# One of three readings of a bit-trick exponential moves from VectorE to GpSimd, with new orders for chunk start, tail and prologue

## The chip, the cores and the metric

The kernel runs on one NeuronCore of a Trainium2 chip. The metric is the device time of one execution in microseconds (us). Engines are named as in the profile: PE (TensorE), DVE (VectorE), ACT (ScalarE), POOL (GpSimd), SP (the engine that issues most DMAs).

## The reference, cut to what matters

```python
xn = layernorm(x)                      # x: 1 x 2048 x 640, no gain, no bias
q = xn @ wq                            # 32 heads of width 20
k, v = xn @ wk, xn @ wv                # one shared key and value head of width 20
p = softmax(q k^T / sqrt(20))          # per head 2048 x 2048, no mask
A = concat_heads(p @ v) @ wo
B = silu(xn @ w1) @ w2                 # hidden width 1728
out = x + A + B                        # bfloat16
```

The 32 x 2048 x 2048 exponentials, 134 million, are the bulk of the elementwise work.

## The kernel before, in words

**Tiling.** The 2048 queries are four chunks (`QC`) of 512 (`QW`). A unit is one head of one chunk; there are 128 units, in 43 groups of three (the last has two). A step is one group against one block of 128 keys, so a group has 16 steps and the kernel 688 (`T`). In a step PE computes the transposed scores (L749): one matmul of 128 keys x 512 queries for each unit, in different row tiles of the array, into three PSUM banks. Two sets of three banks alternate with the step's parity, so step t cannot start before the exponentials of step t-2 have read their banks.

**Two kinds of exponential.** ACT takes exp of the first two units of a step in one instruction (L767, 128x1024, PSUM to a ring of 31 blocks in SBUF). The third unit is either done by ACT too (then the instruction is 128x1536) or, in what is called a DVE step here, by a bit trick on DVE. The scores arrive scaled and offset such that, rounded to int16, they are the bits of a bfloat16 near the exponential. L781, named `p1`, clamps them to 0..32512 and stores int16 in Z. This piecewise linear exponential is read three times at shifted phases and the readings are averaged: Z itself, Z + 43 and Z + 86 (`PH`), all three reinterpreted as bfloat16. The two sums are written to Y by L842, one instruction for each sum over up to three blocks of Z (`ZB`), issued by `flush_z`; the weights of the three readings are folded into copies of V. `want_dve` (from step 8 on) chooses the kind: a step is a DVE step if the backlog of DVE, as the planner has it, is below `DVE_TH`.

**P times V.** L830 multiplies V with the exponentials into one PSUM bank (bank 6), 32 rows for each unit, four column tiles side by side: units 0 and 1, the first reading of unit 2, and its second reading. A step that is all ACT leaves the fourth place free, and `host` gives it to one waiting third reading. Other third readings are collected by threes into extra instruction blocks (`PT`) of four matmuls. At the end of a group DVE copies the bank to SBUF (L945), a DMA transposes it, four small POOL operations add its parts (L912, L915, L917 twice), DVE takes the reciprocal (L922), and POOL multiplies (L931).

**The other work** runs as jobs in bank 7 between the steps: `h_job` (L1057; one hidden block of the FFN, then tanh on ACT L1065 and a multiply on DVE L1070), `out_job` (L1119 is x W2 of the FFN, L1124 is the product with wo, whose results DVE adds in L1136, L1142 or L1148), and `qd_job` (L1023; queries for the next chunk, spread to their places by DMAs). `fill_chunk` lists the jobs of a chunk: the output products of the chunk before it (`fs`), the hidden blocks (`hs`), the FFN output blocks (`ys`), with a query job after every second one, and gives each a first step, spread evenly. Jobs are taken in this order, the head of the list alone. The `fs` read the transposed attention output of the chunk before, which `try_oT` requests by DMA when its last head is done.

**Who sets the order.** `Sched` is a planner that runs while the kernel is built: it simulates the five engines with a time for every operation, commits the order of each engine, and emits semaphore waits. On the chip each engine runs its list strictly in order. `lock` makes the planner keep POOL's group operations and L842 apart in its own time; no semaphore enforces it. `step` chooses PE's next work: scores when ready, else P times V or a job. `fill` inserts matmuls on zeros (L673, L686) when PE has room and its recent busy share is below `FILL_BELOW`.

**Prologue.** x arrives in 16 tiles, mean and variance come from DVE (L1352) or, for tiles in `ACT_STATS`, from ACT; a Newton iteration gives 1/sigma; `norm` normalizes (L1377 on DVE or POOL, L1372 on ACT, by `NORM_ENG`); tiles in `DT` are transposed by DMA on SP's queue (L1430), the others by PE (`tr_job`, L1450) with an evacuation by DVE (L1461). `PRO` lists the order of transposes (t), keys (k), values (v) and queries (q, d). Fourteen DVE operations of 128x512 (L1441) fill the query tiles with their offset.

**Tail.** After the last step come the remaining P times V blocks, a small transpose on PE (L957), the last products with wo for four row tiles in halves (L1124), PE's transposes of the last 128 attention columns (L1097) with an evacuation (L1102), eight matmuls (L1124) and eight additions on DVE (L1148), each pair followed by an output DMA (L1152). The output buffer `ost` has three slots; the last row tile takes the slot of the third before it.

Of the kernel before, what the change touches and what calls it, by code (L numbers as in the profile page):

```python
# [47 lines left out]
ZB = 3  # L48
ZWAIT = 6
SWITCH = 0.105  # L50
S_LEAD = 0.56
PV_PRESS = 8
DVE_TH = 3.2
# [4 lines left out]
FILL_BELOW = 0.78  # L58
OVER = 0.1
FLUSH_G = 0  # L60
NOD = 0
PV_HOLD = 11
# [267 lines left out]
class Job:  # L330
    def __init__(self, name, mms, reads, consume, gate=None, min_step=-1, banks=None, on_start=None, width=0):
# [8 lines left out]
        self.width = width  # L340


class Builder:
# [17 lines left out]
    def alloc(self):  # L361
# [41 lines left out]
        self.eps = sb([P, 1], F32)  # L403
        self.zero = sb([P, 512], BF16)
# [27 lines left out]
    def steps_init(self):  # L432
# [26 lines left out]
        self.nqd = 0  # L459
        self.thirds = []  # L460
# [17 lines left out]
    def bank_for_job(self, job=None):  # L478
        if not self.started and (job is None or job.name[0] != "v"):
# [5 lines left out]
        if self.s_next >= self.T and not self.pv_q:  # L485
            banks = [7, 0, 1, 2, 3, 4, 5]
# [62 lines left out]
    def step(self, now):  # L549
# [54 lines left out]
        nxt = min(sr, pv_r, job_r)  # L604
        if choice is None:
# [26 lines left out]
        else:  # L632
            if job is None:
                job = cand.popleft()
                job.bank = self.bank_for_job(job)[1]
                self.cur_job = job
            self.do_mm(job, now, d)
# [11 lines left out]
    def fill(self, now, until):  # L649
# [7 lines left out]
        if room < 0.08 or self.busy_share(now) > FILL_BELOW:  # L657
# [49 lines left out]
    def do_mm(self, job, now, d):  # L707
# [4 lines left out]
        op.work = work  # L712
# [7 lines left out]
    def want_dve(self, t):  # L720
        if t < DVE_FROM or t % KT >= KT - NOD:
# [8 lines left out]
    def do_S(self, t, now):  # L730
# [42 lines left out]
        if dv:  # L773
# [9 lines left out]
            sc.new("dve", t_dve_ps(QW), p1, [("B", bb)], [("Z", zs, zp)], prio=1.0, name=f"p1_{t}")  # L783
        first = kt == 0
# [48 lines left out]
    def flush_z(self):  # L833
# [7 lines left out]
        for k in range(2):  # L841
            sc.new("dve", t_dve_4x(w), lambda v, k=k: v.tensor_scalar(  # L842
# [264 lines left out]
    def out_job(self, c, i, e, step=-1, ffn=True, ks=range(DC), src="xres", dst="ost", hmax=H):  # L1107
# [14 lines left out]
        for k in ks:  # L1122
            def f(pe, b, k=k, m=len(mms)):
                return pe.matmul(self.bk(b, 0, 320), self.oT[:, k, i * P:(i + 1) * P],  # L1124
                                 self.wo[:, k, e0:e0 + 320], start=(m == 0), stop=(m == tot - 1))
            mms.append((t_mm(320), f))

        def consume(b):
            ps = self.bk(b, 0, 320)
            rk = ("xres", i, e) if src == "xres" else ("yx", i, e)  # L1130
            in1 = (self.xres if src == "xres" else self.yx)[:, i, e0:e0 + 320]
# [15 lines left out]
            sl = n % 3  # L1147
# [440 lines left out]
```

The softmax here doesn't subtract the row's maximum and nothing guards it: scores larger than these inputs give would overflow.

## Time and profile before

| what | us |
|---|---|
| median of 3 runs (743.72 to 744.91) | 744.6 |
| the profiled execution, its own time | 747.35 |
| its span from first to last instruction | 745.6 |
| PE, DVE, ACT, POOL busy | 721.1, 713.9, 707.9, 111.7 |
| first exponential starts | 15.7 |
| last exponential ends | 733.3 |

Busy times are those of the records. Records of one engine overlap: a 128x1024 exponential has a record of 1.08 us, and the next instruction starts 0.905 us after it. So three engines that are all busy 95% of the time may still have room, and where this matters the spacing from start to start is used, read from the trace's start times.

### The profile page before, as it was taken

To read this page: it belongs to the slowest core of one execution; us is meant where nothing else is said; L and a number is where in the kernel's file an instruction comes from. 1 tells how busy PE (TensorE), PEld (TensorE's weight loads), DVE (VectorE), ACT (ScalarE), POOL (GpSimd) and SP (SyncE) were. 2 spreads that over 40 slices of the span, in tenths; PEclk is the share of its full clock that TensorE was granted. 3 is DMA by queue.
4 is the path that set the end of the run, shared out by engine and by line. 5 is a ranking of instruction groups with operands and counts; after the bars stand their busy time and mean duration, and the time that the engine had idled before them with its cause. 6 is when DMAs were issued, how large, how long until landed. Compare 5 with 4: busy or idle time off the path is not lost.

```text
span 745.6 us, 17784 instructions
## 1 busy us (share of the span) xinstructions
PE 721.1 (97%) x6781; PEld 230.5 (31%) x6781; DVE 713.9 (96%) x1397; ACT 707.9 (95%) x780; POOL 111.7 (15%) x280
## 2 busy tenths in 40 slices
PE   8889999999999999999999999999999999999996
PEld 4332222233332222223333232222333322233332
DVE  7978999999999999999999999999999999999997
ACT  8968999999999999999999999999999999999962
POOL 5421112011112111110120111111111121111100
PEclk9979999999999999999999999999999999999999
DMA  6660000101003110000011211000002110000021
GB/s 188 158 248 15 17 20 16 22 16 15 9 15 62 52 46 16 9 16 1 8 16 25 70 44 37 16 8 8 10 8 43 51 45 8 8 9 8 9 43 36
DMA packets 55961, 27.05 MB, mean 36 GB/s; under 512 B 43686, under 2 KB 55238, under 8 KB 55878
## 3 DMA queue, kind: packets, MB, share of 16 engines
q1 hardware_dynamic: 54566, 25.87, 13.7%
q8 instruction: 55, 0.90, 0.5%
q10 hardware_dynamic: 1312, 0.05, 0.1%
q14 instruction: 28, 0.23, 0.1%
HBM read 11.36 MB, written 2.62 MB: 19 GB/s over the span
## 4 chain that ended last, share of the span: by engine, by line
PE 51%; DVE 20%; ACT 19%; issue 5%; POOL 2%; DMA 2%; DVEq 0%; ACTq 0%; POOLq 0%; SPq 0%
ACT sbt L767 18%; PE psall L830 17%; PE psall L749 17%; DVE sbt L781 9%; PE psall L1057 6%; PE psall L1119 5%; DVE sbt L842 5%; PE psall L1023 2%; PE psall L1124 2%; PE psall L673 2%; DVE sbt L1070 1%; DMA sbt<-sbt 1%; ACT sbt L1065 1%; DVE sbt L945 1%; DVE sbt L1352 1%
## 5 line engine op out<-in xcount | busy, mean ns | idle before, releaser
L767 ACT ACTIVATE sbt<-psall 128x1024 bf16<-128x1024 f32 (+2 forms) x688 | 674.4, 1117 | 21.7 <-PE psall L749 18.1
L781 DVE TENSOR_SCALAR sbt<-psall 128x512 int16<-128x512 f32 x608 | 406.4, 684 | 16.5 <-PE psall L749 10.2
L749 PE MATMUL psall<-sbt 32*128 32x512 bf16 x2048 | 269.5, 385 | 12.0 <-ACT sbt L767 6.0
L830 PE MATMUL psall<-sbt 128*32 128x512 bf16 x3434 | 264.7, 387 | 0.0
L842 DVE TENSOR_SCALAR sbt<-sbt 128x1536 int16<-128x1536 int16 (+2 forms) x436 | 223.9, 533 | 1.5
L749 PEld LDWEIGHTS psall<-sbt 32*128 32x128 bf16 x2048 | 69.7, 91 | 252.8 <-issue 86.8
L830 PEld LDWEIGHTS psall<-sbt 128*32 128x32 bf16 x3434 | 67.2, 95 | 112.4 <-issue 75.1
L915 POOL CAST sbt<-sbt 128x168 f32<-128x168 bf16 x42 | 17.3, 411 | 522.0 <-DMA sbt<-sbt 522.0
L1119 PE MATMUL psall<-sbt 128*128 128x320 bf16 x448 | 86.8, 303 | 0.0
L1057 PE MATMUL psall<-sbt 128*128 128x512 bf16 (+1 forms) x280 | 83.6, 384 | 1.6 <-DVE sbt L1070 1.0
L1119 PEld LDWEIGHTS psall<-sbt 128*128 128x128 bf16 x448 | 34.0, 97 | 43.4 <-issue 34.8
L1070 DVE SCALAR_TENSOR_TENSOR sbt<-sbt,psall 128x512 bf16<-128x512 bf16 (+1 forms) x56 | 38.2, 682 | 1.6 <-ACT sbt L1065 0.8
L931 POOL TENSOR_TENSOR sbt<-sbt 128x240 bf16<-128x240 f32 (+2 forms) x44 | 27.9, 635 | 65.7 <-DVE sbt L922 51.1
L1065 ACT ACTIVATE sbt<-psall 128x512 bf16<-128x512 f32 (+1 forms) x56 | 37.6, 671 | 0.0
L1124 PE MATMUL psall<-sbt 128*128 128x320 bf16 x160 | 31.6, 303 | 1.0 <-DVE sbt L1102 0.7
L1057 PEld LDWEIGHTS psall<-sbt 128*128 128x128 bf16 (+1 forms) x280 | 19.6, 98 | 41.3 <-issue 23.3
L945 DVE CAST sbt<-psall 128x512 bf16<-128x512 f32 x43 | 29.4, 684 | 0.9 <-PE psall L830 0.9
L1023 PE MATMUL psall<-sbt 128*128 128x512 bf16 (+1 forms) x95 | 28.4, 385 | 0.0
L917 POOL TENSOR_TENSOR sbt<-sbt 128x44 f32<-128x44 f32 x84 | 26.9, 320 | 6.6
L673 PE MATMUL psall<-sbt 128*32 128x512 bf16 (+9 forms) x86 | 26.6, 389 | 0.0
L912 POOL TENSOR_TENSOR sbt<-sbt 128x84 f32<-128x84 bf16 x42 | 18.0, 429 | 0.0
L1124 PEld LDWEIGHTS psall<-sbt 128*128 128x128 bf16 x160 | 12.0, 97 | 16.6 <-issue 11.7
(85 smaller groups left out, 198.4 us busy)
## 6 DMA issues: line engine op xcount, KB each, us to landing
sbt<-in_A_x_dram SPq DMA_DIRECT2D x32, 160.0 KB, 3.5
out_dram<-sbt SPq DMA_DIRECT2D x16, 160.0 KB, 1.8
sbt<-in_B_w_dram SPq DMA_DIRECT2D x5, 432.0 KB, 5.3
sbt<-sbt SPq DMA_DIRECT2D x105, 20.0 KB
sbt<-in_B_w_dram SPq DMA_DIRECT2D x13, 160.0 KB, 3.7
sbt<-sbt SPq DMA_TRANSPOSE x67, 2.5
sbt<-in_A_wo_dram SPq DMA_DIRECT2D x5, 160.0 KB, 6.1
sbt<-in_A_wq_dram SPq DMA_DIRECT2D x5, 140.0 KB, 3.6
```

Of the source, the lines that this page charges most:

```text
L673: return pe.matmul(self.bk(UBANK, 0, n, 0, 32), self.zero[:, 0:32], self.zero[:, 0:n], start=False, stop=False, tile_position=(0, 0), skip ...
L749: ins = pe.matmul(self.bk(par3 + j), self.kT[r:r + SLOT, kk, kt * P:(kt + 1) * P], self.qT[r:r + SLOT, h // 4, (x // H) % 2, :], start=Tru ...
L767: return a.activation(self.E[:, b0 * QW:(b0 + na) * QW], self.ps[:, par3 * BANK:(par3 + na) * BANK], AF.Exp, scale=ACT_SCALE)
L781: return v.tensor_scalar(self.Z[:, zs, zp * QW:(zp + 1) * QW], self.bk(bb), 0.0, ZMAX, ALU.max, ALU.min)
L830: return pe.matmul(self.bk(UBANK, 0, QW, q * SLOT, (q + 1) * SLOT), self.v[:, w, kt, :], x, start=start, stop=stop, tile_position=(0, q * ...
L842: sc.new("dve", t_dve_4x(w), lambda v, k=k: v.tensor_scalar(self.Y[:, zs, k, 0:n * QW], Z, float(PH[k + 1][0]), None, ALU.add), zk, [("Y", ...
L1023: return pe.matmul(self.bk(b, 0, QW, 0, rows), self.wq[:, k, lo:hi], self.xnT[:, k, c * QW:(c + 1) * QW], start=(k == 0), stop=(k == DC - 1))
L1057: return pe.matmul(self.bk(b, 0, QW, 0, rows), self.w1[:, k, fk * P:fk * P + rows], self.xnT[:, k, c * QW:(c + 1) * QW], start=(k == 0), s ...
L1065: sc.new("act", t_act(QW), lambda a: a.activation(t, src, AF.Tanh, scale=0.5), [("B", b)], [("tb", tp)], prio=X_PRIO, name=f"th{c}_{fk}")
L1070: sc.new("dve", t_dve_ps(QW), lambda v: v.scalar_tensor_tensor(out=self.hT[0:rows, fk, :], in0=t, scalar=1.0, in1=src, op0=ALU.add, op1=AL ...
L1119: return pe.matmul(self.bk(b, 0, 320), self.hT[0:rows, fk, i * P:(i + 1) * P], self.w2[0:rows, fk, e0:e0 + 320], start=(m == 0), stop=(m = ...
L1124: return pe.matmul(self.bk(b, 0, 320), self.oT[:, k, i * P:(i + 1) * P], self.wo[:, k, e0:e0 + 320], start=(m == 0), stop=(m == tot - 1))
```

## The change

1. **Third reading.** The sum Z + 86 is no longer the second instruction of `flush_z`. For each DVE step POOL adds the int32 constant 86 x 65537 to Z read as 256 int32 words a partition (two packed int16 values each; the clamp leaves no carry), as soon as `p1` is done. The planner counts 0.72 us for it, without `lock`, and 0.1 us more for each L842 that remains.
2. **Chunk start.** `fill_chunk` puts four hidden blocks ahead of the output products of the chunk before (`H_FIRST`).
3. **Tail.** P times V goes first in the last 16 steps (`LASTPV`), the last step is no DVE step. For row tiles 2 and 3 a new `hold_job` collects x + FFN by two matmuls with the identity and four of the five products with wo in PSUM banks of their own; the last product goes to the same bank, and ACT evacuates it with a factor of 0.5. Row tiles 0 and 1 go as before; the two kinds alternate. The transposes of the last 128 columns are urgent. The last row tile has an output slot of its own and its DMA goes out on ACT's queue.
4. **Prologue.** New lists `PRO`, `DT`, `ACT_STATS`, `NW_ENG`, `NORM_ENG`. The fourteen L1441 become one POOL operation and two SP DMAs that copy its row 6 and 8 times, ahead of the loads of w1 and wo. The planner counts less PE activity for transposes and value products, and fills below a busy share of 0.95 in the first 64 steps.
5. **Constants**: `DVE_TH`, `PV_PRESS`, `PV_HOLD`.

```diff
+Y_POOL = True
+Y_TIME = 0.72
+Y_LOCK = False
+Y_SLOW = 0.1
+H_FIRST = 4
+NEARLY = 2
+LASTPV = 16
+DVE_LAST = 1
 ZWAIT = 6
 SWITCH = 0.105
 S_LEAD = 0.56
-PV_PRESS = 8
-DVE_TH = 3.2
+PV_PRESS = 12
+DVE_TH = 2.8
 U_PRIO = 1.1
 X_PRIO = 0.8
 PACE = (0.9, 0.9, 0.9, 0.9)
 WIN = 3.4
 FILL_BELOW = 0.78
+FILL_EARLY = 0.95
+FILL_STEPS = 64
 OVER = 0.1
 FLUSH_G = 0
 NOD = 0
-PV_HOLD = 11
+PV_HOLD = 9
 Q_EVERY = 2
 DT_ISSUE = 1.28
 UT_ISSUE = 1.05
-DT = (4, 5, 6, 7, 11, 12, 13, 14, 15)
-NORM_P = 0.05
+DT = (4, 5, 8, 9, 10, 11, 12, 13, 14, 15)
+NORM_P = 0.5
 DVE_FROM = 8
-PRO = "v0 t8 t9 k2 t10 k3 k4 k5 q1 v1 k6 k7 d0 v2 v3"
-ACT_STATS = (2, 4, 6, 8, 9, 12)
-NW_ENG = ("dve", "pool", "pool", "dve")
-NORM_ENG = ("dve", "act", "dve", "dve", "pool", "pool", "dve", "act", "dve", "pool", "act", "act")
+PRO = "t6 v0 k2 t7 k3 k4 q1 v1 v2 k5 k6 k7 v3 d0"
+ACT_STATS = (4, 6, 9, 12, 14)
+NW_ENG = ("dve", "pool", "dve", "pool")
+NORM_ENG = ("pool", "pool", "pool", "pool", "dve", "act", "act", "dve", "act", "dve", "dve", "act")
...
+        if job is not None and job.use is not None:
+            return 0.0, self.heldb[job.use]
         if not self.started and (job is None or job.name[0] != "v"):
             banks = [7, 6, 5, 4, 3]
         elif not self.pv_started:
             banks = [7, 6]
         else:
             banks = [7]
-        if self.s_next >= self.T and not self.pv_q:
-            banks = [7, 0, 1, 2, 3, 4, 5]
+        if self.s_next >= self.T:
+            banks = [b for b in (7, 0, 1, 2, 3, 4, 5) if b not in self.heldb.values()]
...
+        if self.s_next >= self.T - LASTPV and pv_n:
+            choice = "PV"
...
-        if room < 0.08 or self.busy_share(now) > FILL_BELOW:
+        if room < 0.08 or self.busy_share(now) > (FILL_BELOW if self.s_next > FILL_STEPS else FILL_EARLY):
...
-        op.work = work
+        op.work = min(work, 0.009) if job.name[0] == "v" else min(work, 0.053) if job.name[0] == "t" else work
...
-        if t < DVE_FROM or t % KT >= KT - NOD:
+        if t < DVE_FROM or t % KT >= KT - NOD or t >= self.T - DVE_LAST:
...
+            self.y_on_pool = Y_POOL
+            if self.y_on_pool:
+                c86 = bass.AP(self.c86, self.c86[:, :].offset, [list(self.c86[:, :].ap[0]), [0, QW // 2]])
+                sc.new("pool", Y_TIME, lambda v: v.tensor_tensor(
+                    self.Y[:, zs, 1, zp * QW:(zp + 1) * QW].bitcast(I32),
+                    self.Z[:, zs, zp * QW:(zp + 1) * QW].bitcast(I32), c86, ALU.add),
+                    [("Z", zs, zp), ("c86",)], [("Y", zs, 1, zp)], prio=4.0, name="yp").lock = Y_LOCK
...
-        for k in range(2):
-            sc.new("dve", t_dve_4x(w), lambda v, k=k: v.tensor_scalar(
+        for k in range(1 if self.y_on_pool else 2):
+            sc.new("dve", Y_SLOW + t_dve_4x(w), lambda v, k=k: v.tensor_scalar(
                 self.Y[:, zs, k, 0:n * QW], Z, float(PH[k + 1][0]), None, ALU.add), zk,
...
-            sl = n % 3
-            sc.new("dve", t_dve_ps(320), lambda v: v.scalar_tensor_tensor(
-                out=self.ost[:, sl, e0:e0 + 320], in0=ps, scalar=0.5, in1=in1, op0=ALU.mult, op1=ALU.add),
-                [("B", b), rk], [("ost", sl, e)], prio=X_PRIO, name=f"out{n}_{e}")
+            sl = n % 3 if n < NT - 1 else 3
+            ost = self.ost[:, sl, :] if sl < 3 else self.hT[:, :, :].rearrange("p a b -> p (a b)")[:, 0:D]
+            wk = [("ost", sl, e)] + ([("hT", 0), ("hT", 1)] if sl == 3 else [])
+            if src == "ps":
+                sc.new("act", t_act(320), lambda a: a.activation(ost[:, e0:e0 + 320], ps, AF.Copy, scale=0.5),
+                       [("B", b)], wk, prio=X_PRIO, name=f"out{n}_{e}")
+            else:
+                sc.new("dve", t_dve_ps(320), lambda v: v.scalar_tensor_tensor(
+                    out=ost[:, e0:e0 + 320], in0=ps, scalar=0.5, in1=in1, op0=ALU.mult, op1=ALU.add),
+                    [("B", b), rk], wk, prio=X_PRIO, name=f"out{n}_{e}")
             if e == 1:
-                op = sc.dma("sp", lambda q: q.dma_start(self.outv[:, n, :], self.ost[:, sl, :]),
+                op = sc.dma("act" if sl == 3 else "sp", lambda q: q.dma_start(self.outv[:, n, :], ost),
                             [("ost", sl, 0), ("ost", sl, 1)], [("outd", sl)], P * D * 2, sem=self.s_out[sl])
                 self.out_cnt[sl] += 1
                 op.inc_no = self.out_cnt[sl]
...
+    def hold_job(self, c, i, e):
+        e0 = 320 * e
+        mms = []
+        for m in range(2):
+            def f(pe, b, m=m):
+                return pe.matmul(self.bk(b, 0, 320), self.idb[:, :], self.xres[:, i, e0:e0 + 320], start=(m == 0),
+                                 stop=False)
+            mms.append((t_mm(320), f))
+        for k in range(DC - 1):
+            def f(pe, b, k=k):
+                return pe.matmul(self.bk(b, 0, 320), self.oT[:, k, i * P:(i + 1) * P], self.wo[:, k, e0:e0 + 320],
+                                 start=False, stop=False)
+            mms.append((t_mm(320), f))
+        return Job(f"G{i}_{e}", mms, [("xres", i, e), ("idb",), ("oT", i), ("oTv", c, i), ("wo",)], lambda b: None,
+                   gate=lambda: self.s_next >= self.T and (c, i, e) in self.y_done, hold=(i, e))
...
-        for n, x in enumerate(fs + hs + ys):
+        for n, x in enumerate(hs[:H_FIRST] + fs + hs[H_FIRST:] + ys):
...
-            for i in range(4):
+            for i in range(NEARLY):
                 for e in range(2):
                     self.misc.append(self.out_job(c, i, e, ffn=False, ks=range(DC - 1), src="yx", dst="yx"))
-            self.misc.append(self.oT_last_job(c))
-            for i in range(4):
+            for i in range(NEARLY, 4):
                 for e in range(2):
-                    self.misc.append(self.out_job(c, i, e, ffn=False, ks=range(DC - 1, DC), src="yx"))
+                    self.misc.append(self.hold_job(c, i, e))
+            self.urgent.append(self.oT_last_job(c))
+            fin = [(i, e) for i in range(4) for e in range(2)]
+            lo = [x for x in fin if x[0] < NEARLY]
+            hi = [x for x in fin if x[0] >= NEARLY]
+            while lo or hi:
+                for x, src in ((hi, "ps"), (lo, "yx")):
+                    if x:
+                        i, e = x.pop(0)
+                        self.misc.append(self.out_job(c, i, e, ffn=False, ks=range(DC - 1, DC), src=src))
 
 
     def prologue(self):
@@ -1228,8 +1286,8 @@
         sem = sc.sem
...
+        pool(0.1, lambda g: g.memset(self.c86[:, :], PH[2][0] * 65537), [], [("c86",)])
...
+        pool(0.95, lambda g: g.tensor_scalar(self.tb[:, 0, :], self.zero[:, 0:QW], self.offq[:, :], 1.0, ALU.add, ALU.mult),
+             [("zero",), ("offq",)], [("tb", 0)])
+        tb = self.tb[:, 0, :]
+        for par in range(2):
+            h0 = 2 if par == 0 else 0
+            rep = bass.AP(self.tb, tb.offset, [list(tb.ap[0]), [0, HT - h0], list(tb.ap[1])])
+            op = sc.dma("sp", lambda q, par=par, h0=h0, rep=rep: q.dma_start(self.qT[:, h0:HT, par, :], rep), [("tb", 0)],
+                        [("qb", par, h) for h in range(4 * h0, H)], P * (HT - h0) * QW * 2, sem=sem(f"qz{par}"))
+            op.inc_no = 1
         load_w("sp", "1", [lambda q, c=c: q.dma_start(self.w1[:, c, :], self.B_w1[c * P:(c + 1) * P, :])
                            for c in range(DC)], ("w1",), P * F * 2)
         load_w("sp", "o", [lambda q, c=c: q.dma_start(self.wo[:, c, :], self.A_wo[c * P:(c + 1) * P, :])
                            for c in range(DC)], ("wo",), P * D * 2)
-        for par in range(2):
-            for ht in range(2 if par == 0 else 0, HT):
-                np_("dve", 0.31, lambda v, par=par, ht=ht: v.tensor_scalar(
-                    self.qT[:, ht, par, :], self.zero[:, 0:QW], self.offq[:, :], None, ALU.add),
-                    [("zero",), ("offq",), ("mv", 3)], [("qb", par, h) for h in range(4 * ht, 4 * ht + 4)],
-                    prio=6.0 + par, name="qz")
-
         def tr_job(n):
             mms = []
```

More of the change, by code (lines that the diff above doesn't have):

```diff
@@ L330, with __init__ @@
 class Job:
-    def __init__(self, name, mms, reads, consume, gate=None, min_step=-1, banks=None, on_start=None, width=0):
+    def __init__(self, name, mms, reads, consume, gate=None, min_step=-1, banks=None, on_start=None, width=0, hold=None, use=None):
         self.name = name
@@ L340, in __init__ @@
         self.width = width
+        self.hold = hold
+        self.use = use
 class Builder:
@@ L403, in alloc @@
         self.eps = sb([P, 1], F32)
+        self.c86 = sb([P, 1], I32)
         self.zero = sb([P, 512], BF16)
@@ L459, in steps_init @@
         self.nqd = 0
+        self.heldb = {}
         self.thirds = []
@@ L636, in step @@
                 self.cur_job = job
+                if job.hold is not None:
+                    self.heldb[job.hold] = job.bank
             self.do_mm(job, now, d)
@@ L1124, in f @@
                 return pe.matmul(self.bk(b, 0, 320), self.oT[:, k, i * P:(i + 1) * P],
-                                 self.wo[:, k, e0:e0 + 320], start=(m == 0), stop=(m == tot - 1))
+                                 self.wo[:, k, e0:e0 + 320], start=(m == 0 and src != "ps"), stop=(m == tot - 1))
             mms.append((t_mm(320), f))
@@ L1129, in consume @@
             ps = self.bk(b, 0, 320)
-            rk = ("xres", i, e) if src == "xres" else ("yx", i, e)
-            in1 = (self.xres if src == "xres" else self.yx)[:, i, e0:e0 + 320]
+            rk = ("yx", i, e) if src == "yx" else ("xres", i, e)
+            in1 = (self.yx if src == "yx" else self.xres)[:, i, e0:e0 + 320]
             if dst == "ost":
@@ L1167, in out_job @@
             gate = lambda: (c, i, e) in self.y_done
-        return Job(f"F{n}_{e}", mms, reads, consume, min_step=step, width=320)
+        return Job(f"F{n}_{e}", mms, reads, consume, gate=gate, min_step=step, width=320,
+                   use=(i, e) if src == "ps" else None)
+    def hold_job(self, c, i, e):
[13 more added lines that the diff above has]
+                   gate=lambda: self.s_next >= self.T and (c, i, e) in self.y_done, hold=(i, e))
     def load_xres(self, c, i):
@@ L1204, in fill_chunk @@
                 for e in range(2):
-                    jobs.append((2.9, lambda s, i=i, e=e: self.out_job(c, i, e, s, ks=(), dst="yx")))
+                    jobs.append((2.9, lambda s, i=i, e=e: self.out_job(c, i, e, s, ks=(), dst="yx" if i < NEARLY else "xres")))
         s0 = self.first_step[c]
@@ L1230, in prologue @@
         self.outv = self.out[0].rearrange("(n p) d -> p n d", p=P)
-        self.s_out = [sem(f"outd{i}") for i in range(3)]
-        self.out_cnt = [0] * 3
+        self.s_out = [sem(f"outd{i}") for i in range(4)]
+        self.out_cnt = [0] * 4
         self.s_UT = [sem(f"UT{i}") for i in range(2)]
```

## The prediction

> **What bounds the kernel now.** I first read the busy shares (PE 97%, DVE 96%, ACT 95%, POOL 15%), which name three candidates and one idle engine, and then the groups of instructions with their shapes kept apart:
>
> ```profile
> L767 ACT ACTIVATE sbt<-psall 128x1024 bf16<-128x1024 f32 x596 | 569.8, 1080 | 11.5 <-PE psall L749 10.5 <-PE psall L830 0.6
> L781 DVE TENSOR_SCALAR sbt<-psall 128x512 int16<-128x512 f32 x608 | 406.4, 684 | 16.5 <-PE psall L749 10.2 <-PE psall L830 3.4
> ...
> L842 DVE TENSOR_SCALAR sbt<-sbt 128x1536 int16<-128x1536 int16 x348 | 190.9, 560 | 1.5
> ...
> L767 ACT ACTIVATE sbt<-psall 128x1536 bf16<-128x1536 f32 x78 | 116.1, 1493 | 3.6 <-PE psall L830 2.4 <-PE psall L749 1.1
> ...
> L842 DVE TENSOR_SCALAR sbt<-sbt 128x1024 int16<-128x1024 int16 x84 | 35.0, 432 | 0.0
> ...
> L931 POOL TENSOR_TENSOR sbt<-sbt 128x240 bf16<-128x240 f32 x40 | 26.4, 659 | 48.9 <-DVE sbt L922 48.9
> ```
>
> The reader is to see that 608 of 688 steps are DVE steps, that in 78 steps ACT does three units, and that half of L842, some 113 us of DVE records, is what the change moves. Next the stretches:
>
> ```profile
> core 0: us, PE busy (x) PEld busy (x) DVE busy (x) ACT busy (x) POOL busy (x), PEclk, DMA share, GB/s
> ...
> 27.00:60.00 33.00, 29.16 (x242) 11.30 (x240) 23.98 (x58) 22.68 (x22) 7.41 (x11) 0.79 0.62 204
> ...
> 424.00:564.00 140.00, 137.89 (x1309) 42.11 (x1305) 136.33 (x254) 139.98 (x153) 17.53 (x40) 1.00 0.08 20
> ...
> 704.00:746.00 42.00, 35.56 (x334) 13.55 (x332) 37.11 (x83) 20.58 (x28) 3.58 (x10) 0.99 0.17 36
> ```
>
> In the middle ACT has no idle time at all: from 60 to 704 us it is the engine that ends last. From start to start an exponential of two units takes 0.905 us, of three 1.331, a tanh 0.478; beyond these ACT loses only about 0.5 us in 28. The start runs PE at a clock of 0.79, and the end leaves ACT idle half the time.
>
> I cut 60 to 704 us into 23 stretches of 28 us: 635 steps, 1.014 us each. Adding up PE's runs at their least start-to-start cost (three scores 0.321 with the switch, four P-times-V matmuls 0.332, eight 0.548, twelve 0.764, two hidden-block matmuls 0.537) gives 603.5 us of PE need, 0.950 a step; fills take 0.030 and waits 0.036. For ACT (539.4 + 103.8 exponentials, 27 tanh, 7 last group) it is 0.984 a step. DVE's spacing is 0.601 for L781 and 0.466 for a three-block L842: 365 + 191 + 105 for all else = 661, or 0.961 a step. So all three stand within 4%; freeing one helps until the next is full.
>
> [...] the trace shows both kinds of waiting:
>
> ```profile
> 357.48 1.37 DVE L842 TENSOR_SCALAR sbt<-sbt 128x1536 int16<-128x1536 int16 x2
> 357.71 0.72 POOL L931 TENSOR_TENSOR sbt<-sbt 128x240 bf16<-128x240 f32 x1 [0.69 <-DVE sbt L922]
> ```
>
> Two L842 should take 1.02 us; here the second has a record of 0.956 instead of 0.551, since POOL got in between. In eleven of the 42 groups POOL's L912 takes about 0.65 instead of 0.343 us beside L842. But others overlap at full speed[...]. [...] with PE busy 7.3 of 10 us at 20 to 30 us and a clock of 0.75 just after.
>
> **The change, part by part.**
>
> *Third reading off DVE.* Half of L842, 191/2 = 95 us of spacing, leaves DVE. On POOL no row shows a 32-bit add. Nearest: two-input operations back to back, 44 elements 0.349 us, 84 elements 0.420, so 1.78 ns an element, and 256 elements 0.73 us. [...] 0.85 us, with an L842's half behind which it waits, is the high end. I take 0.73. POOL then has per step 0.73, plus 2.1/16 = 0.13 of group operations (0.285 + 0.420 + 2 x 0.35 + 0.67), 0.86 of about 1.0: it fits[...]. DVE in turn waits for POOL: nothing to 0.40 us (the case above) on each of some 226 L842; I take 0.15.
>
> *More DVE steps.* With this room `want_dve` says yes almost always: 679 steps instead of 608 (8 at the start, one at the end excluded). ACT: 71 x 0.426 = 30 us less, 0.984 to 0.940 a step. DVE: 408 + 107 + 34 of waits + 105 = 654, 0.951. PE: a DVE step has a third reading more and no free place. About 70 of 608 thirds were hosted, the others made some 190 extra blocks; now 16 thirds a group make five full blocks and one part, 42 x 6 = 252. 62 x 0.216 = 13.4 us, or 0.020 a step: PE's need goes to 0.970. **PE is next.** What falls out of its 1.014 are the fills (0.030) and part of the waits, since ACT and DVE have slack now. Bounds: waits of 0.005 to 0.036. I take 0.022: 0.992 a step. On 662 steps (60 to 732 us) that is 662 x 0.022 = 14.6 us. The changed `PV_PRESS`, `PV_HOLD` and `DVE_TH` move run lengths both ways; I count nothing, and the bounds above cover it.
>
> *Hidden blocks first.* At a chunk's start the output products wait for a transpose that needs the last head's P times V; the steps at 200 to 228 us show the hole (fills 3.5 us, need 23.3 of 28). Work is moved, none added; the gain of up to 3 x 2 us is in the fills that I have removed already. Tanh and L1070 come with the blocks, four of 56, earlier.
>
> *Prologue.* Fourteen L1441 (3.6 us of DVE spacing) go. In their place: one POOL operation, 0.5 to 1 us, and two DMAs of 0.79 and 1.05 MB on SP ahead of w1 and wo. At the 286 to 345 GB/s of 30 to 50 us they take some 6 us. w1 landed at 40.1 and is first used at 60.4, w2 at 50.3 and 153.9: they are hidden; without that cover the hidden blocks would start 6 us late. Queries that overwrite these tiles are sent from 46.9 us, past the landing. One tile less through PE (5 transposes 0.43, evacuation 0.39 on DVE), one more DMA transpose on SP (1.3 us of issue); one tile less in ACT's statistics (-1.5 us), one more in DVE's (+0.9); POOL normalizes four tiles in a row, 4 x 0.88 = 3.5 us, and two of these PE transposes wait for. [...] 29.2 us of PE at 0.79 instead of 1.0 is 6 us at most, if nothing else were late; only 26 steps are done by 60 us, and DVE and ACT have 9 and 10 us of slack at 28 to 56 us. I take 3 us, bounds 0 and 6.
>
> *Tail.*
>
> ```profile
> 736.55 1.79 PE L1124 MATMUL psall<-sbt 128*128 128x320 bf16 x12
> ...
> 738.18 0.39 PE L1097 MATMUL psall<-sbt 128*128 128x128 bf16 x4
> ...
> 739.61 2.48 DVE L1148 SCALAR_TENSOR_TENSOR sbt<-psall,sbt 128x320 bf16<-128x320 f32 x6 [0.40 <-PE psall L1124]
> ...
> 742.44 0.89 DVE L1148 SCALAR_TENSOR_TENSOR sbt<-psall,sbt 128x320 bf16<-128x320 f32 x2 [0.35 <-DMA out_dram<-sbt]
> ```
>
> The transposes stand behind twelve products although their input was done at 737.4: 0.6 us. The eight additions end at 743.33, PE's last matmul at 740.5. With four on ACT and a slot of its own for the last tile, the end comes at about 741.2: 2.1 us. Eight identity matmuls (1.1 us) go into PE's wait. The last L842 are halved but POOL's sum adds 0.73. Together 3 us, bounds 1.5 and 4.5.
>
> Sum: 14.6 + 3 + 3 = 20.6. Span 745.6 - 20.6 = 725.0; with the 1.75 us around it 726.7; the profiled execution is 2.75 above the median, so **724.0 us**.
>
> **The rivals.**
>
> *A, the forecast:* PE takes over at about 0.992 a step. 716 to 733.
>
> *B, PE eats the gain.* The extra blocks come in full and the waits stay at 0.036, PE being in order and the score banks only two sets deep: 1.006, a gain of 5, and 3 from the tail, 0 at the start: 744.6 - 8 = **736.6**. For it: stretches without fills already show need up to 0.99 a step.
>
> *C, everything packs.* Waits of 0.005: 26, start 6, tail 4: **708.6**. Against it: three engines would have to run at 97% with a depth of two.
>
> *D, slower: [...].* If a hold covers the whole of POOL's 0.73 and nothing of L842 hides, a step needs 0.73 + 0.13 + 0.155 = 1.015 [...], and a DVE step's L781 can't run ahead more than four Z sets. With 0.045 more for handing over, two waits a flush, it is 1.06: 662 x 0.046 = 30 slower, less 6 for start and tail: **768.6**. It decides from 1.023 a step on, that is, from 0.74 us for the add under full exclusion. For it: both waits in the trace. Against: overlaps at full speed, with L842 at 0.55 beside 0.5 us of POOL.
>
> That the sums don't move at all can't be; that no more steps go to DVE is within B.
>
> **How the numbers follow.** A 0.54, B 0.20, C 0.09, D 0.15; 0.02 for gains that cancel. The predicted time is A's. The range runs from C's 709 to past B, 740; left out are D and a half of C. A measurement of this kernel tells 0.2% (1.5 us) from no change. A, B and C, less 0.01 of B, are faster: 0.82; same 0.03; slower 0.15.
>
> **What would show it.** Right: L842 near 226 and a POOL line near 679 of spacing 0.7 to 0.8; about ten three-unit exponentials; ACT with idle time in the middle while PE's fills vanish there; L830 some 3600 matmuls instead of 3434; a higher clock at 27 to 60; the last addition within 6 us of the last P-times-V copy. Wrong: L842 with records well above 0.7 us, POOL busy over 90%, and PE waiting for POOL's sums (D); ACT still without idle time and three-unit exponentials still frequent (the room was not used); fills and waits unchanged (B).

## The result and the profile after

The changed kernel takes **739.6 us** (739.08 to 741.28), the kernel before 744.75 in the same session: a ratio of 0.9937 with an interval of 0.9917 to 0.9957. The forecast said 724.0. The sign is right, the size is not: 5.2 us instead of 20.6. The profiled execution took 740.04 us, its span is 738.2.

The groups of instructions of the changed kernel, with shapes kept apart (count; busy us and mean ns; idle time before and its releasers):

```profile
L787 ACT ACTIVATE sbt<-psall 128x1024 bf16<-128x1024 f32 x632 | 597.4, 1077 | 10.9 <-PE psall L769 10.4
L807 POOL TENSOR_TENSOR sbt<-sbt 128x256 int32<-128x256 int32 x646 | 447.2, 698 | 149.3 <-DVE sbt L801 122.7 <-PE psall L769 9.8 <-PE psall L857 2.5
L801 DVE TENSOR_SCALAR sbt<-psall 128x512 int16<-128x512 f32 x646 | 432.5, 683 | 34.4 <-PE psall L769 26.4 <-POOL sbt L944 1.0 <-POOL sbt L939 0.4
...
L869 DVE TENSOR_SCALAR sbt<-sbt 128x1536 int16<-128x1536 int16 x198 | 119.1, 602 | 2.7
...
L787 ACT ACTIVATE sbt<-psall 128x1536 bf16<-128x1536 f32 x41 | 60.8, 1489 | 2.6 <-PE psall L769 2.5
```

(The exponential is now L787, `p1` L801, the sums on DVE L869, the sum on POOL L807, scores L769, P times V L857, products with W2 L1146.) The change did what it says: 646 DVE steps instead of 608, 41 three-unit exponentials instead of 78, half of the L842 gone. The stretches:

```profile
core 0: us, PE busy (x) PEld busy (x) DVE busy (x) ACT busy (x) POOL busy (x), PEclk, DMA share, GB/s
27.00:60.00 33.00, 28.84 (x302) 11.57 (x302) 25.99 (x57) 27.39 (x28) 17.87 (x32) 0.98 0.88 267
...
424.00:564.00 140.00, 137.32 (x1347) 41.35 (x1355) 132.19 (x230) 140.00 (x156) 108.47 (x182) 1.00 0.12 26
704.00:739.00 35.00, 30.66 (x239) 16.12 (x237) 17.81 (x38) 7.69 (x14) 8.32 (x15) 0.99 0.07 24
```

In the middle DVE has room (132 of 140 us instead of 136), and ACT still has none. In the last 35 us ACT is busy for 7.7 us, where before it had 20.6 in 42. The start times of the exponentials show where that comes from:

| stretch of the span | before | after | difference |
|---|---|---|---|
| to the start of step 64 | 100.6 | 100.9 | +0.3 |
| step 64 to step 687 | 632.1 | 611.2 | -20.9 |
| start of the last step to the end of its exponential | 0.6 | 1.0 | +0.4 |
| from there to the end of the program | 12.2 | 25.1 | +12.9 |
| sum: the span | 745.6 | 738.2 | -7.3 |

The steps alone gained as much as was forecast for the whole kernel: 1.015 us to 0.981 each, where the forecast had 0.992. Then 12.9 us came back behind the last exponential. Its timeline (start, us, engine, line):

```profile
712.08 1.02 ACT L787 ACTIVATE sbt<-psall 128x1024 bf16<-128x1024 f32 x1 [0.68 <-PE psall L769]
...
717.46 10.61 PE L1146 MATMUL psall<-sbt 128*128 128x320 bf16 x70
728.00 2.35 PE L1151 MATMUL psall<-sbt 128*128 128x320 bf16 x16
...
733.78 1.56 ACT L1178 ACTIVATE sbt<-psall 128x320 bf16<-128x320 f32 x4 [20.68 <-PE psall L1151]
```

86 products with W2 start after the last exponential, before none did. At 0.136 us from start to start these are 11.7 of the 20.68 us for which ACT idles.

The first exponentials gained nothing, although the clock at 27 to 60 us rose from 0.79 to 0.98 and 30 steps instead of 26 were done by 60 us. There is a hole at 60 to 67 us (SPq is SP's queue, here the issue of a transfer):

```profile
56.68 1.28 SPq L931 DMA_TRANSPOSE sbt<-sbt  x1
...
62.01 0.33 POOL L942 CAST sbt<-sbt 128x168 f32<-128x168 bf16 x1 [3.93 <-DMA sbt<-sbt]
...
64.27 0.23 DVE L949 RECIPROCAL sbt<-sbt 128x12 f32<-128x12 f32 x1 [3.73 <-POOL sbt L944]
...
65.82 1.47 PE L857 MATMUL psall<-sbt 128*32 128x512 bf16 x12 [2.02 <-DVE sbt L869]
...
67.94 1.94 ACT L787 ACTIVATE sbt<-psall 128x1024 bf16<-128x1024 f32 x2 [5.45 <-PE psall L769]
```

The transpose of the first group's result stands on SP behind the loads, which now have 1.8 MB of copies ahead of them: w1 lands at 51.4 us instead of 40.1, w2 at 61.5 instead of 50.3. POOL waits for the transpose, DVE for POOL, PE for DVE, ACT for PE: one transfer, told four times. It lands at 62.0 us, no later than before (63.2); but the exponentials had got four steps ahead, and here they lose that lead: between the starts of steps 31 and 32 pass 7.0 us, before 2.2. What stands behind a waiting instruction waits too: in this trace all 1206 records of DVE start in the order of its list, and so do the 760 of ACT, the 924 of POOL and 6407 of the 6408 of PE that can be placed in theirs.

### The profile page after: what moved, and what is told of

Same layout as the page of the kernel before. It is cut to its first block, busy times and chain, and to the rows that moved or that the text cites. A ratio compares the mean times of both kernels' runs of the same rounds, so it can differ in the third digit from the quotient of the medians.

```text
span 738.2 us, 18883 instructions
## 1 busy us (share of the span) xinstructions
PE 707.6 (96%) x6798; PEld 229.7 (31%) x6852; DVE 665.5 (90%) x1206; ACT 691.0 (94%) x780; POOL 538.4 (73%) x929
## 4 chain that ended last, share of the span: by engine, by line
PE 62%; ACT 17%; DVE 6%; issue 5%; POOL 1%; DMA 1%; DVEq 0%; ACTq 0%; POOLq 0%
PE psall L857 21%; PE psall L769 20%; ACT sbt L787 15%; PE psall L1146 9%; PE psall L1084 6%; DVE sbt L801 3%; PE psall L1151 2%; PE psall L1050 2%; ACT sbt L1092 1%; DVE sbt L869 1%; DMA sbt<-sbt 1%; DVE sbt L972 1%; PE psall L693 1%; POOL sbt L807 0%; DVE sbt L1057 0%
## 5 line engine op out<-in xcount | busy, mean ns | idle before, releaser
L787 ACT ACTIVATE sbt<-psall 128x1024 bf16<-128x1024 f32 (+2 forms) x688 | 657.8, 1091 | 16.8 <-PE psall L769 15.9
L807 POOL TENSOR_TENSOR sbt<-sbt 128x256 int32<-128x256 int32 x646 | 447.2, 698 | 149.3 <-DVE sbt L801 122.7
L801 DVE TENSOR_SCALAR sbt<-psall 128x512 int16<-128x512 f32 x646 | 432.5, 683 | 34.4 <-PE psall L769 26.4
L769 PE MATMUL psall<-sbt 32*128 32x512 bf16 x2048 | 269.1, 385 | 9.7 <-ACT sbt L787 4.7
L857 PE MATMUL psall<-sbt 128*32 128x512 bf16 x3524 | 270.2, 385 | 4.2 <-DVE sbt L869 2.0
L769 PEld LDWEIGHTS psall<-sbt 32*128 32x128 bf16 x2048 | 68.7, 91 | 252.8 <-issue 105.1
L869 DVE TENSOR_SCALAR sbt<-sbt 128x1536 int16<-128x1536 int16 (+2 forms) x230 | 134.8, 587 | 2.8
L857 PEld LDWEIGHTS psall<-sbt 128*32 128x32 bf16 x3524 | 67.8, 94 | 115.0 <-issue 75.4
L1146 PE MATMUL psall<-sbt 128*128 128x320 bf16 x448 | 86.2, 302 | 0.0
L1084 PE MATMUL psall<-sbt 128*128 128x512 bf16 (+1 forms) x242 | 75.7, 385 | 5.1 <-issue 3.7
L1146 PEld LDWEIGHTS psall<-sbt 128*128 128x128 bf16 x448 | 35.1, 97 | 43.4 <-issue 33.8
L1084 PEld LDWEIGHTS psall<-sbt 128*128 128x128 bf16 (+1 forms) x280 | 18.8, 98 | 39.9 <-issue 29.6
L1151 PE MATMUL psall<-sbt 128*128 128x320 bf16 x144 | 28.7, 303 | 0.4 <-DVE sbt L1181 0.4
L1050 PE MATMUL psall<-sbt 128*128 128x512 bf16 (+1 forms) x81 | 26.6, 385 | 2.4 <-issue 1.4
L706 PE MATMUL psall<-sbt 128*128 128x512 bf16 (+2 forms) x67 | 17.5, 407 | 4.8 <-DVE sbt L1565 3.3
L942 POOL CAST sbt<-sbt 128x168 f32<-128x168 bf16 x42 | 14.2, 337 | 9.7 <-DMA sbt<-sbt 9.1
```

The source lines that it names most:

```text
L769: ins = pe.matmul(self.bk(par3 + j), self.kT[r:r + SLOT, kk, kt * P:(kt + 1) * P], self.qT[r:r + SLOT, h // 4, (x // H) % 2, :], start=Tru ...
L787: return a.activation(self.E[:, b0 * QW:(b0 + na) * QW], self.ps[:, par3 * BANK:(par3 + na) * BANK], AF.Exp, scale=ACT_SCALE)
L801: return v.tensor_scalar(self.Z[:, zs, zp * QW:(zp + 1) * QW], self.bk(bb), 0.0, ZMAX, ALU.max, ALU.min)
L807: sc.new("pool", Y_TIME, lambda v: v.tensor_tensor(self.Y[:, zs, 1, zp * QW:(zp + 1) * QW].bitcast(I32), self.Z[:, zs, zp * QW:(zp + 1) * ...
L857: return pe.matmul(self.bk(UBANK, 0, QW, q * SLOT, (q + 1) * SLOT), self.v[:, w, kt, :], x, start=start, stop=stop, tile_position=(0, q * ...
L869: sc.new("dve", Y_SLOW + t_dve_4x(w), lambda v, k=k: v.tensor_scalar(self.Y[:, zs, k, 0:n * QW], Z, float(PH[k + 1][0]), None, ALU.add), z ...
```

## The experiments

Each kernel is timed in five rounds against the kernel before (744.9 to 745.1 us); ratios are to that.

**Which part of the change does it?** Third reading back to DVE, all else as changed:

```diff
-Y_POOL = True
+Y_POOL = False
-Y_SLOW = 0.1
+Y_SLOW = 0.0
```

> The changed kernel, but the third reading stays on DVE as the second L842. Theory (the steps got some 20 us faster by the third reading, PE then fills up and FFN products are left for the end, and a hole at 60 us in the new prologue costs about 6): the steps fall back by 20 us, the left-over FFN products at the end vanish (-12), so 745 to 750 us, last exponential near 733. Rival 1 (waits of DVE and POOL [...] ate the gain): the time does not rise, 736 to 741. Rival 2 (the 5 us come from the new job order and tail alone): 738 to 741.

Measured: 752.0 us, 1.0087 [1.0069, 1.0104], 2 us beyond what was expected: 585 DVE steps, 99 three-unit exponentials, and one product with W2 after the last of them. And the third reading alone, in the kernel before:

```diff
+            sc.new("pool", 0.72, lambda v: v.tensor_tensor(
...
-        for k in range(2):
-            sc.new("dve", t_dve_4x(w), lambda v, k=k: v.tensor_scalar(
+        for k in range(1):
+            sc.new("dve", 0.1 + t_dve_4x(w), lambda v, k=k: v.tensor_scalar(
```

> The kernel before, with the third reading on POOL (0.72 us in the planner, 0.1 more for each L842) and nothing else of the change. Theory: the steps end some 15 to 20 us earlier, FFN products are left over at the end, no hole at 60 us: 735 to 741 us. Rival 1 [...]: 744 or more, with L842 spacings above 0.55 us. Rival 2 (job order and tail bring the gain): 743 to 746.

Measured: 744.9 us, 0.9998 [0.9986, 1.0009]: a miss. DVE takes 669 steps and the last exponential ends at 721.9 instead of 733.3, but 42 products with W2 come after it and the tail is 19.6 us. Its steps fell only to 1.003 us, which isn't explained. So moving the third reading is worth nothing by itself, the rest costs 7, and together they gain 5: the parts don't add. Most edits reorder all of the planner's list, so single differences of 1 to 3 us are not to be put down to the edited line alone.

**Is PE the bound?** Both kernels with half of the products with W2 left out (7 of 14 a block, so part of the FFN sum is missing; 30 us of PE less).

```diff
-            for fk in range(FC):
+            for fk in range(FC // 2):
```

> The kernel before, with 7 of the 14 products of the FFN's second matmul left out in every output block: 224 matmuls of 0.135 us, 30 us of PE work less, ACT and DVE work unchanged. Theory (before, ACT and DVE set the pace and PE has room): 741 to 744 us, PE fills instead. Rival 3 (PE's work was the bound already before): 715 to 722 us.

> The changed kernel, with 7 of the 14 products of the FFN's second matmul left out in every output block: 30 us of PE work less, ACT and DVE work unchanged. Theory (with the third reading away, PE's whole work sets the end; what the steps gain comes back as FFN products after the last step): 12 to 16 us below the changed kernel, 724 to 728, with about 40 products and no more after the last step, where the same cut in the kernel before brought 2.7. Rival ([...] ACT set the end as before): at most 4 us below, 735 to 739.

Measured: the kernel before 742.2, 0.9966 [0.9951, 0.9981], only 2.7 less; the changed one 726.7, 0.9758 [0.9746, 0.9771], 12.9 less. In the latter the last exponential still ends at 713.6, no product comes after it (about 40 were expected), and the tail is 11.3 us. This pair is the clearest: 30 us of PE work hide behind ACT in the kernel before, and 13 of them are the end of the changed one.

**Can more DVE steps help?** `DVE_TH` at 9 gives 679, the forecast's count.

> The changed kernel with DVE_TH at 9, so that all 679 steps that may be DVE steps are. That is the number which the forecast assumed. Forecast's reasoning: ACT falls to 0.94 a step, PE at 0.97 is next, 730 or less. Theory (PE is full): the last exponential comes at about 700 instead of 713, 30 more third-reading blocks and more left-over FFN products bring the end to 741 to 746. Rival [...]: L842 spacing above 0.55 us, and steps no faster than 646 DVE steps make them.

Measured: 744.1, 0.9987 [0.9977, 0.9998]. Its groups and stretches:

```profile
L787 ACT ACTIVATE sbt<-psall 128x1024 bf16<-128x1024 f32 x665 | 623.0, 1064 | 12.1 <-PE psall L769 11.4
...
L787 ACT ACTIVATE sbt<-psall 128x1536 bf16<-128x1536 f32 x8 | 11.3, 1444 | 1.9 <-PE psall L769 1.9
```

```profile
core 0: us, PE busy (x) PEld busy (x) DVE busy (x) ACT busy (x) POOL busy (x), PEclk, DMA share, GB/s
...
700.00:745.00 45.00, 39.25 (x253) 22.14 (x252) 18.53 (x37) 7.67 (x15) 0.85 (x2) 0.99 0.17 49
```

The last exponential ends at 700.2, 13 us earlier than in the changed kernel, and 44 us follow it, with ACT idle for 37 of the last 45: 112 products with W2 and some hidden blocks. A step is 0.0207 us shorter than in the changed kernel, and ACT's need by the 33 fewer three-unit exponentials 0.0204. Steps that ACT runs faster leave less time for the jobs that run between them.

**POOL's add beside DVE's sums.** The POOL sum is cut to 2 of 256 words, with the order of all engines unchanged; the third reading takes the second's sums, so Z + 86 is left out.

```diff
-                    self.Y[:, zs, 1, zp * QW:(zp + 1) * QW].bitcast(I32),
+                    self.Y[:, zs, 1, zp * QW:zp * QW + 4].bitcast(I32),
...
-            x = self.Y[:, zs, 1, i * QW:(i + 1) * QW].bitcast(BF16)
+            x = self.Y[:, zs, 0, i * QW:(i + 1) * QW].bitcast(BF16)
```

> The changed kernel with the same order on every engine, but POOL's sum covers 2 of the 256 words of a block, and the third reading takes the second's sums: Z + 86 is left out, PE's work is the same. It takes away POOL's 0.7 us [...]. Rival (waits [...] for late sums cost the expected gain): 727 to 733. Theory ([...] PE's work sets the end): 736 to 739, L842's successor back to a spacing of 0.47 us.

Measured: 738.0, 0.9900 [0.9883, 0.9917]. Its groups:

```profile
L807 POOL TENSOR_TENSOR sbt<-sbt 128x2 int32<-128x2 int32 x646 | 180.3, 280 | 396.5 <-DVE sbt L801 330.5 <-PE psall L769 36.7 <-PE psall L857 5.6
...
L869 DVE TENSOR_SCALAR sbt<-sbt 128x1536 int16<-128x1536 int16 x198 | 110.0, 556 | 2.8
```

From start to start a three-block L869 takes 0.474 us here and 0.527 in the changed kernel: waiting beside POOL's whole adds costs 0.05 us each, 10 us of DVE in all. The time is 1.6 us shorter (the two intervals just touch), with POOL's shorter sum included.

Who waits is seen in the changed kernel's trace. The 330 adds that no sum of DVE's overlaps have records of 604 to 618 ns. In none of the 215 pairs of an add and a three-block sum that overlap by 0.2 us or more do both have their usual length: in 129 the add alone is longer, in 40 the sum alone, in 46 both. Here two adds, 1.18 us when nothing hinders them, take 1.50 beside a sum of 0.68 instead of 0.55:

```profile
56.59 1.50 POOL L807 TENSOR_TENSOR sbt<-sbt 128x256 int32<-128x256 int32 x2 [0.61 <-DVE sbt L801]
...
56.93 0.68 DVE L869 TENSOR_SCALAR sbt<-sbt 128x1536 int16<-128x1536 int16 x1
```

**The start.** The query tiles filled by DVE as before (the first list), the whole old prologue (the second), and only the longer of the two copies moved behind the first query DMAs on SP, with a source of its own (the third):

```diff
-        pool(0.95, lambda g: g.tensor_scalar(self.tb[:, 0, :], self.zero[:, 0:QW], self.offq[:, :], 1.0, ALU.add, ALU.mult),
...
+                np_("dve", 0.31, lambda v, par=par, ht=ht: v.tensor_scalar(
```
```diff
-PRO = "t6 v0 k2 t7 k3 k4 q1 v1 v2 k5 k6 k7 v3 d0"
+PRO = "v0 t8 t9 k2 t10 k3 k4 k5 q1 v1 k6 k7 d0 v2 v3"
...
```
```diff
+        sp.remove(self.qz1)
+        sp.insert([i for i, o in enumerate(sp) if o.name == "qdma"][6] + 1, self.qz1)
```

> The changed kernel, but the query tiles are filled by the fourteen DVE operations again, not by two DMAs on SP. Theory (the hole at 60 to 67 us is there because these 1.8 MB push the weight loads and with them the transpose of the first group back, on which DVE's reciprocal and all behind it waits): the loads land about 9 us earlier, the hole closes, 733 to 736 us. Rival (the hole has another cause, or PE's total work sets the end anyway): 739 to 742, since DVE gets 3.6 us of work back.

> The changed kernel with the prologue of before (its lists, query tiles filled by DVE, PV_HOLD, fills and PE activity counted as before). The third reading alone reached step 64 at 96.3 us with that prologue, the changed kernel at 100.9. Theory (the new prologue loses 4 to 5 us on the chip): 734 to 737. Rival (it gains its 3 us as predicted, and the 96.3 came from DVE_TH): 742 to 745. If PE's whole work is all that counts: 739 to 741.

> The changed kernel with the same order on every engine but SP's: the larger of the two DMAs that fill query tiles (1.05 MB, for the second chunk) goes out after the first query DMAs at about 63 us, not ahead of w1 at 38. Theory (the hole at 60 to 67 us is the first group's transpose landing late behind the weight loads): the loads land about 4 us earlier, step 64 comes at 97 to 98 instead of 100.9, and the end comes 1 to 3 us earlier, 736.5 to 738.5. Rival (PE's whole work is all that counts and is merely moved): 739 to 740.

Measured: 742.2, 0.9959 [0.9946, 0.9971]; 741.9, 0.9952 [0.9940, 0.9964]; 738.1, 0.9904 [0.9889, 0.9918]. In the first the gap before step 32 shrinks from 7.0 to 3.6 us, but 3.3 us are lost between steps 8 and 16, after the fourteen operations on DVE (that they are the cause is likely, not shown), and step 64 starts at 101.7: a miss. w1 lands at 45.8 here: the copies hold it back by 5.6 us, and the other 5.7 against the kernel before come with the new lists, under which SP has issued its transposes only at 36.7 instead of 31.4. In the second step 64 starts at 97.2, 3.7 earlier, and nothing of it arrives: 100 products stand after the last exponential and the tail is 27.6 us, also a miss. In the third the transpose lands at 59.6 instead of 62.0, the gap is 3.5 us, step 64 starts at 98.8 and 1.5 us of the 2.1 arrive (the intervals just touch). What then holds the scores of step 32 (L772 here) is another transfer of the same queue, the last of the query DMAs, which lands at 65.55:

```profile
65.59 0.12 PEld L772 LDWEIGHTS psall<-sbt 32*128 32x128 bf16 x6 [0.85 <-DMA sbt<-sbt]
```

So the longer copy makes half of the hole, and is worth some 1.5 us.

**The tail and the chunk start**, each put back alone:

```diff
-NEARLY = 2
-LASTPV = 16
-DVE_LAST = 1
+NEARLY = 4
+LASTPV = 0
+DVE_LAST = 0
```
```diff
-H_FIRST = 4
+H_FIRST = 0
```

> The changed kernel with the tail of before as far as it goes (all four last row tiles by DVE, no P-times-V priority in the last 16 steps, the last step may be a DVE step; the urgent transposes and the output slot stay). Theory (the tail's shared evacuation saves the 2 to 3 us that were predicted, hidden by the left-over products): 741 to 743. Rival (the new tail costs, since P times V first pushes FFN products behind the last step): 735 to 738.

> The changed kernel with H_FIRST at 0: the output products of the chunk before lead again. Theory (the order of jobs moves idle time of PE within the chunk and adds no work; every constant reshuffles the plan by a few us): 739 to 743. Rival (the hole at a chunk's start is what the change gained): 744 or more.

Measured: 740.1, 0.9937 [0.9925, 0.9949], both expectations missed, since no difference from the changed kernel can be seen; and 741.1, 0.9946 [0.9933, 0.9959], as expected, but within the interval of the changed kernel too. With the old tail the last exponential ends 3.5 us later and 49 products follow instead of 86. PE's last matmul starts at 732.7 instead of 734.5, and the end comes 5.3 us after it instead of 3.7: what the new evacuation gains, PE's longer way there costs.

**Why does PE idle while jobs wait?** The planner keeps a job away from PE if it would end more than `OVER` past the time at which scores are due (`S_LEAD` before the exponential ends), and no job begins before a first step spread by `PACE`.

```diff
-OVER = 0.1
+OVER = 0.3
```
```diff
-S_LEAD = 0.56
+S_LEAD = 0.36
```
```diff
-PACE = (0.9, 0.9, 0.9, 0.9)
+PACE = (0.75, 0.75, 0.75, 0.75)
```

> The changed kernel, but the planner may let a job or a P-times-V block run up to 0.3 us past the time at which the next scores are due (OVER, before 0.1). Theory G, PE idles in the middle because this guard keeps work away from it ahead of the scores: PE's waits and fills from 60 us on fall from 37.6 to below 30 us, W2 products after the last exponential from 86 to below 55, the last exponential ends a few us later, and the time is 733 to 738 us. Theory F, the work is held back by the first steps given to jobs (PACE): nothing changes but the order, 739 to 742 us. Theory K, ACT and PE are both full and what one gives the other loses: fewer products after, but the exponentials later by as much, 739 to 742 us.

> The changed kernel, but scores are due 0.36 us ahead of the end of the exponential before them, not 0.56 us (S_LEAD). Theory G: as OVER does, PE's waits fall, fewer products are left, 734 to 739 us. Theory K: ACT gets its scores later and loses what PE gains, 739 to 743 us. Theory F: no change beyond the order, 739 to 742 us.

> The changed kernel with OVER 0.6 instead of 0.1, so that scores hardly hold any work back. Theory G: waits and fills of PE below 22 us, fewer than 30 W2 products after the last exponential; 730 to 738 us. Theory K: products after the end vanish, but ACT waits for scores in the middle and the last exponential ends near 724 us: 737 to 743 us.

> The changed kernel with the first steps of all jobs spread over 0.75 of a chunk, not 0.9 (PACE). Theory F, jobs are held back by their first steps: fewer than 40 W2 products after the last exponential and 731 to 736 us. Theories G and K: jobs lag behind their first steps already and wait for room on PE, so 80 to 100 products are left and the time is 738 to 742 us.

Measured: 746.0, 1.0017 [1.0006, 1.0027]; 746.2, 1.0025 [1.0014, 1.0036]; with `OVER` 0.6 748.1, 1.0032 [1.0020, 1.0044]; `PACE` 739.9, 0.9934 [0.9922, 0.9946]. Two of the four are repeats: with `PACE` 0.75 the planner gives every engine the same order as in the changed kernel, since jobs lag behind their first steps anyway, and `OVER` 0.6 the same order as 0.3, since at 0.3 the guard holds nothing back that 0.6 would let pass; the repeats lie 0.3 and 2.1 us from the first measurements. The first three are slower than every theory had it. SP's queue in the first of them shows a part of the reason:

```profile
50.18 7.75 SPq L1326 DMA_DIRECT2D sbt<-in_B_w_dram  x14
58.03 3.20 SPq L1066 DMA_DIRECT2D sbt<-sbt  x4
61.29 1.24 SPq L931 DMA_TRANSPOSE sbt<-sbt  x1
```

Earlier jobs send query DMAs ahead of the first group's transpose, which goes out at 61.29 instead of 56.68 and lands at 64.9 instead of 62.0; the hole grows by far more, and step 32 starts at 79.7 instead of 67.9. Three jobs, one after the other in bank 7, now stand on PE ahead of its scores, from 68.3 to 77.1 us; this wasn't taken apart. Behind the hole the comparison is clean. From step 48 to 687 `OVER` 0.3 puts 40 more products with W2 between the steps, 40 x 0.136 = 5.4 us, and the steps take 631.2 us instead of 627.2. PE's waits and fills there are 43.5 us against 42.6 (both traces lack some 50 matmul records, which read as about 12 us of waits in each). A product moved in between the steps thus saves 0.136 us at the end and costs the steps 0.10; with `S_LEAD` 0.36, which moves 57, it costs 0.12. The guard isn't what leaves PE idle; ACT and PE give each other most of what they take.

**The best version:** the changed kernel with the old prologue, `DVE_TH` 2.9, `PV_PRESS` and `PV_HOLD` 10, `LASTPV` 8, `H_FIRST` and `DVE_LAST` 0:

```diff
-H_FIRST = 4
+H_FIRST = 0
...
-DVE_TH = 2.8
+DVE_TH = 2.9
```

> The changed kernel with the prologue of before and other constants (DVE_TH 2.9, PV_PRESS 10, H_FIRST 0, LASTPV 8, DVE_LAST 0, PV_HOLD 10), which in the planner's own times ends as early as the changed kernel does, while the old prologue lost less between plan and chip. Theory: 736 to 738. Rival (the new prologue is worth its 2.3 us everywhere): 740 to 743.

Measured: **736.1 us**, 0.9877 [0.9860, 0.9894], as expected, and faster than both kernels: 653 DVE steps, the last exponential at 711.5, 71 products after it, PE's fills down to 6.1 us and its waits still at 25.9.

## Why the prediction was wrong, step by step

**The step that failed** is "PE is next ... I take 0.022": the idle time that PE keeps. In the forecast's accounting from 60 us on (runs at their least cost, fills, waits), PE had 631.4, 19.9 and 27.9 us before and has 634.3, 11.1 and 26.5 after. These are read from the kernel with POOL's sum cut short, whose order is the same: the changed kernel's own trace lacks 52 matmul records of L1084 and L1050, which would read as waits. (Least costs chosen a little differently move some 3 us from waits to runs, in both kernels alike.) Over the forecast's 662 steps idle is 0.057 a step, not 0.022: the fills were halved, the waits stayed. That is 19 us less saved than the forecast had (10.2 of 662 x 0.044 = 29). PE's need rose by 2.9 us, not 13.2, which gives back 10; part of this is that four more steps lie ahead of 60 us, and part that P times V has 3524 matmuls, not some 3600 (with all 679 DVE steps it has 3619, so the count itself was right). The forecast's net, 29 less 13.2 (14.6 with its own rounding), thus became 10.2 less 2.9 = 7.3 there. In the changed kernel itself, with POOL's whole sums, PE's last matmul starts at 734.5 instead of 740.2, 5.7 us earlier, and the end comes 3.7 us after it instead of 5.3. These 5.7 and 1.6 are the 7.3 us by which its span is shorter; 13.3 of the 20.6 are missing. The start's 3 are among them: step 64 starts 0.3 us later. The other 2.1 are the two profiled executions: 2.75 us above its median before, 0.45 after.

**The mean over the span hid the order.** The forecast applied one rate to 662 steps and let jobs spread with them. ACT still sets the pace: 0.905 + 41/688 x 0.426 + 0.039 for the rest = 0.969 of 0.981 us a step, and from 100 to 690 us it idles for 1.1 us in all. What the steps gained, PE's jobs lost, and they come after the last exponential. Of the rivals B is nearest (736.6, waits unchanged), but not in its place: it had the steps slow at 1.006. That the 739.6 lies within the forecast's range, at its very end of 740, is no success of the mechanism. Of its signs the 230 sums (226) and the higher clock came; ACT without idle time, 41 three-unit exponentials instead of about ten, and 21 us instead of 6 from the last P-times-V copy to the last addition spoke against it.

**More DVE steps:** 646, not 679, since `DVE_TH` is lower (9 gives 679; what the 0.1 us more for each remaining sum does alone wasn't tried). It was no loss: with 679 the time is 744.1.

**POOL's add:** 0.73 taken. The records have 698 ns in the mean, waits beside DVE included; from start to start, one add behind another, it is 0.571 (median of 127), 0.16 less than taken. **DVE's wait for POOL:** 0.15 us on each sum taken, 0.05 measured. None of the 215 overlapping pairs runs unhindered; what the two engines share then, the traces don't show. It is mostly POOL that waits, 86 ns an add in the mean (698 against 612), and POOL has time. The forecast's "others overlap at full speed" was a wrong reading: in the kernel before, too, none of 88 pairs from 60 us on that overlap by 0.2 us or more has both at their usual length, and the POOL operations of 0.5 us beside an L842 of 0.55 take 0.27 or 0.33 alone. Rival D, in which the add, POOL's other work and the sums (0.155 a step, a third of 0.466) never overlap, is excluded by the steps of 0.981 us and because cutting the sum short saved only 1.6 us. By its own sum it needed a long add: its threshold of 0.74 us leaves out the 0.045 for handing over that its 1.06 has, and is 0.69 with it; 0.571 is below both. The 0.045 was the author's estimate; in the trace of before, the shortest times from the end of an L922 on DVE to the start of POOL's L931 are 0.079 us, and two of these a flush of three steps would be 0.053 a step.

**Hidden blocks first:** counted at nothing beyond the fills; putting them back can't be told from no change. **Prologue:** "w1 and w2 are hidden" was true, and the 6 us for the copies were right (5.6), but the new lists cost the loads as much again, and the transfers next on the same queue were not looked at: the first group's transpose and the query DMAs. The clock at 27 to 60 us rose as expected (0.79 to 0.98), but step 64 starts no earlier (100.9 instead of 100.6). That the fills raised it isn't shown: with only the third reading moved, and fills as before, no fortieth of the span has a clock below 0.9 either. **Tail:** 3 us taken. Its largest part, 2.1 for the shared evacuation, came to 1.6: the end is 3.7 to 3.8 us behind the start of PE's last matmul in the kernels with the new tail (4.5 in one of them) and 5.2 to 5.4 in those with the old. But the identity matmuls (1.1 us) did not go into a wait of PE's: with half of the products with W2 left out of both kernels, so that none stand in the way, PE's last matmul starts 7.5 us after the last exponential instead of 6.3, and the tail is 11.3 us against 11.6.

**What stays open:** what PE's 26 us of waits between 60 us and the end are made of. First steps and the guard don't cause them. Half of them, some 12 us, stand right ahead of scores, whose weight loads wait most often for an exponential of ACT's (166 times, 63.9 us in all; next comes DVE's L801 with 108 times and 42.7 us); that scores must wait for one of two sets of banks fits this, but that, and one bank for all jobs, is argued, not shown. Removing them would need another use of the PSUM banks, which wasn't tried.

## What to carry to other kernels

When an engine is relieved, ask of every other engine not only how much work it has in the mean but whether it can still be done before the last instruction of the one that sets the pace: here 86 products with W2 that had run in the shadow of slower steps came out behind the last exponential. A test that removes half of the shadowed work from both kernels (2.7 us before, 12.9 after) showed which one is bound by it. And a transfer added to a queue can be paid by a short transfer that stands behind it, not only by its own reader: with the longer copy moved back, the first group's transpose landed at 59.6 us instead of 62.0.

## What the runs showed of the hardware that was not expected

POOL's int32 add of 256 words takes 0.571 us from start to start, the same add of 2 words 0.147 (medians of 127 and of 13 that follow one another): by these two, as an estimate, a quarter of it (0.144 us) doesn't depend on the size. Their mean records, 698 and 280 ns, hold waits beside DVE and would put it at 40%. In none of 215 meetings with a sum of DVE's did both run unhindered, yet DVE's sums lose only 0.05 us on average beside a POOL that is busy 73% of the time (0.474 to 0.527 from start to start), since in most meetings it is the add that waits. Single sums had waited 0.4 us in the trace of before.
